# One load for the first modulation weights, fewer warm-up matmuls, a cast moved ahead of statistics, and a branch hint in a fused attention and MLP block

## The chip, the cores and the metric

One core of a Trainium2 chip. The metric is the device time of one execution in microseconds; each kernel was run several times. Executions of one kernel agree to about 0.1%, which is 1 us here (nine of the kernel before in one round: 1328.14 to 1329.20 us), and the whole change is about effects of that size. So two things are used throughout: runs of the kernel before made in the same rounds on the same chip, and the trace, in which a shift can be followed step by step.

## The reference, cut to what matters

```python
mod = (silu(c) @ w_mod).reshape(1, 6, 1, 512)        # sa, ca, ga, sb, cb, gb
h = layernorm(x) * (1 + ca) + sa                     # x: 1 x 2048 x 512
q = h @ wq                                           # 32 query heads of 128
o = softmax(q @ k.T * 128**-0.5) @ v                 # 8 KV heads, 2048 keys, from a cache
x = x + ga * (o @ wo)
h = layernorm(x) * (1 + cb) + sb
x = x + gb * mlp(h)                                  # GELU, layernorm, spatial gate, 512 -> 1792 -> 512
```

Inputs and output are bfloat16. The scores can be exponentiated without a running maximum as long as they are small; a flag computed on the way says whether that holds, and a branch at the end goes to a general path when it does not. In these runs the flag is zero and the branch jumps over that path.

## The kernel before

The change touches the first 25 us and the last matmul. The first loads: the first two of the six modulation parts (`wmod_a`, 1 MB) come in two halves, then half of K for the first head, then `wq` of the first group and the next three row tiles of x. ACT's queue issues `c` and the first row tile.

```python
    c_bf = res.tile([P, NDT], BF16, name="c_bf")
    nc.scalar.dma_start(out=c_bf[:], in_=c_dram)
    nc.scalar.dma_start(out=x_sb[:, 0, :], in_=x_dram[:, 0, :])
    for i in range(2):
        part = slice(i * D, (i + 1) * D)
        nc.sync.dma_start(out=wmod_a[:, :, part], in_=wmod_dram[:, :, part])
    k_nat = early.tile([P, SK], BF16, name="kT")
    nc.sync.dma_start(out=k_nat[:, 0:HK].rearrange(...), in_=k_rows)
    # ... (cut)
    load_wq(0, nc.sync)
    nc.sync.dma_start(out=x_sb[:, 1:CT, :], in_=x_dram[:, 1:CT, :])
```

The first row tile. `warm(n)` issues n matmuls of zeros, 128x512, which serve nothing but TensorE's clock. `mod_columns` is 32 matmuls of one column. `ln1_turn` transposes the normalised rows on TensorE and applies the modulation on DVE and ACT (the result is `hT`). `qproj` is the query projection: 16 matmuls, then a cast from PSUM to `qT`, half on DVE and half on ACT for this first tile.

```python
    warm(14)
    xns0 = ln1_norm(0, 1, ln1_stats(0, 1))
    mod_columns(0, wmod_a, 0)
    ln1_turn(0, 1, xns0, on_act=(1, 3))
    # ... K transposed on TensorE into kT0 (cut)
    warm(2)
    first = {}
    first["r1"] = ln1_stats(1, 1)
    # ... (cut: definition of qproj)
    for fn in qproj(0, list(range(REP)), 0, P, two_engines=True):
        fn()
    first["x1"] = ln1_norm(1, 1, first["r1"])
    first["r2"] = ln1_stats(2, 2)
```

Then comes the attention loop, one slot for each pair of score matmuls of 512 columns with an exponential of 1024 columns behind it. Work of the next row tiles is placed into slots by number: `at` runs it at a slot, `fill` puts matmuls between.

```python
    def first_turn():
        ln1_turn(1, 1, first["x1"])
        first["x2"] = ln1_norm(2, 2, first["r2"])

    at(0, 1, first_turn)
    at(0, 4, lambda: ln1_turn(2, 2, first["x2"]))
    fill[0, 0] = [lambda: warm(1)]
    fill[0, 2] = [lambda: warm(1)]
    fill[0, 3] = qproj(0, list(range(REP)), P, P)
    rest_q = qproj(0, [0, 1], 2 * P, 2 * P) + qproj(0, [2, 3], 2 * P, 2 * P)
    fill[0, 6], fill[0, 7], fill[1, 0] = rest_q[0:4], rest_q[4:10], rest_q[10:16]
```

## Time and profile before

| | before |
|---|---|
| time, median of 3 runs | 1328.81 us (1328.66 to 1328.84) |
| profiled span | 1326.9 us |
| TensorE busy | 98% of the span |
| granted clock, mean | 0.998 |
| first query projection | 9.62 to 10.69 us |
| first score matmul | 12.33 us |
| last of the early casts of qT | 22.98 us |

How to read the profile: PE is TensorE (PEld its weight loads), DVE VectorE, ACT ScalarE, POOL GpSimd, and SP SyncE, for which the page lists no busy time: here it issues and waits; PSUM is the memory in which the results of the matmuls lie. An engine is seen here to take its instructions in order, so one that waits holds up all behind it: the cast at 11.48 stood behind statistics, though its projection had ended at 10.69. Each line of the timeline has the start, the length, the engine, the source line, the operation with what it writes and reads, the number of instructions, and in brackets the idle time before it with what ended it. Matmuls of one group overlap in the trace (one of 512 columns is shown 0.38 us long, two 0.59); their spacing tells the clock: those of 512 columns start 427 ns apart in the warm-up before and 215 ns apart at the first score matmuls, those of 128 columns 107 and 56 ns. The lines on which the argument rests are in the prediction below.

### The profile page before, as it was taken

Reading aid. Unit: us, or ns where it says so; the run is one execution under the profiler, and the core shown is the slowest. Engines: PE = TensorE matmul, PEld = TensorE weight load, DVE = VectorE, ACT = ScalarE, POOL = GpSimd, SP = SyncE. Lnnn points to the kernel's source line nnn. Section 1 sums busy time; section 2 is a strip of 40 time slices with the busy share of each in tenths; the row PEclk is TensorE's granted clock in tenths of the full one; section 3 lists DMA queues with packets and bytes.
Section 4 is the critical chain, followed back from the end, with each engine's and each line's share of the span. In section 5 each row is a group of like instructions: output and inputs, shape, how many; then the busy total and the mean of one; then the engine's idle time right before and its main releaser. Section 6 shows DMA issues by size and latency. Waiting matters only on the chain.

```text
span 1326.9 us, 27682 instructions
## 1 busy us (share of the span) xinstructions
PE 1303.0 (98%) x12140; PEld 859.3 (65%) x12346; DVE 472.7 (36%) x1166; ACT 1077.4 (81%) x1061; POOL 48.8 (4%) x92
## 2 busy tenths in 40 slices
PE   8999999999999999999999999999999999999997
PEld 5666666666666666666666666666666666644444
DVE  5532222222222222222222222222222566793444
ACT  5898999999999999999999999999999999650000
POOL 1100000000000000000000000000000000120000
PEclk9999999999999999999999999999999999999999
DMA  5461021102111121111110211121101111154200
GB/s 159 102 146 29 17 49 37 33 17 53 21 30 36 34 37 37 29 37 37 33 33 17 53 37 29 21 52 21 33 14 21 25 34 33 29 115 83 64 21 27
DMA packets 146512, 57.59 MB, mean 43 GB/s; under 512 B 136176, under 2 KB 142448, under 8 KB 146384
## 3 DMA queue, kind: packets, MB, share of 16 engines
q1 hardware_dynamic: 139584, 37.19, 14.8%
q0 software_dynamic: 4208, 16.39, 4.5%
q8 instruction: 98, 1.61, 0.5%
q10 hardware_dynamic: 2592, 2.16, 0.5%
q14 instruction: 30, 0.25, 0.1%
HBM read 21.37 MB, written 2.10 MB: 18 GB/s over the span
## 4 chain that ended last, share of the span: by engine, by line
PE 97%; issue 1%; DVE 1%; DMA 1%; ACT 0%; SPq 0%; POOL 0%
PE s_ps L928 35%; PE o_ps L950 35%; PE misc L1290 7%; PE misc L889 7%; PE misc L982 6%; PE s_ps L1136 2%; PE s_ps L1175 2%; PE o_ps L1311 1%; DMA x_sb<-in_A_x_dram 1%; PE s_ps L1311 0%; DVE bnst L691 0%; ACT pT L935 0%; PE misc L1052 0%; DVE qT L901 0%; DVE xn L680 0%
## 5 line engine op out<-in xcount | busy, mean ns | idle before, releaser
L935 ACT ACTIVATE pT<-s_ps 128x1024 bf16<-128x1024 f32 x1024 | 1043.6, 1024 | 86.0 <-PE s_ps L928 11.3
L950 PEld LDWEIGHTS <-pT 128*128 128x128 bf16 x8192 | 548.5, 98 | 241.2
L950 PE MATMUL o_ps<-v,pT 128*128 128x129 bf16 x8192 | 631.5, 220 | 0.0
L928 PE MATMUL s_ps<-qT,kT 128*128 128x512 bf16 x2048 | 608.9, 379 | 12.4 <-ACT qT L903 1.6
L961 DVE RECIPROCAL rall<-o_ps 128x2 f32<-128x2 f32 x256 | 43.6, 170 | 743.9 <-PE o_ps L950 743.8
L928 PEld LDWEIGHTS <-kT 128*128 128x128 bf16 x2048 | 199.3, 98 | 121.8 <-issue 3.6
L889 PE MATMUL misc<-hT,wq_g 128*128 128x512 bf16 (+2 forms) x482 | 167.4, 365 | 0.2
L982 PE MATMUL misc<-wo_g,oT 128*128 128x512 bf16 x385 | 145.9, 379 | 0.0
L962 DVE TENSOR_TENSOR onorm<-o_ps,rall 128x256 bf16<-128x256 f32 x256 | 108.6, 424 | 9.0 <-DVE rall L961 0.3
L1290 PE MATMUL misc<-wsp,z 128*128 128x512 bf16 (+2 forms) x555 | 100.5, 336 | 0.6 <-issue 0.3
L901 DVE CAST qT<-misc 128x512 bf16<-128x512 f32 (+1 forms) x128 | 86.7, 677 | 7.4 <-PE misc L889 7.3
L1290 PEld LDWEIGHTS <-z 128*128 128x128 bf16 x560 | 50.6, 98 | 48.5
L995 DVE TENSOR_TENSOR xacc<-misc,xacc 128x512 f32<-128x512 f32 x112 | 76.0, 679 | 0.0
L889 PEld LDWEIGHTS <-wq_g 128*128 128x128 bf16 x544 | 51.5, 98 | 1.5 <-DMA wq_g<-in_A_wq_dram 0.6
L982 PEld LDWEIGHTS <-oT 128*128 128x128 bf16 x512 | 50.1, 98 | 0.7
L1305 DVE TENSOR_TENSOR gb<-misc,bsp_bc 128x512 bf16<-128x512 f32 (+1 forms) x28 | 18.4, 658 | 59.2 <-PE misc L1290 59.2
L1136 PE MATMUL s_ps<-win_sb,hT 128*128 128x448 bf16 x128 | 27.0, 352 | 0.1
L1146 ACT ACTIVATE z<-s_ps 128x896 bf16<-128x896 f32 x16 | 14.7, 917 | 14.9 <-PE s_ps L1136 14.9
L1175 PE MATMUL s_ps<-hT,win_sb 128*128 128x512 bf16 x109 | 24.3, 379 | 0.2
L691 DVE BATCH_NORM_STATS2 bnst<-x_sb 128x6 f32<-128x512 bf16 x32 | 21.8, 682 | 3.1 <-DMA x_sb<-in_A_x_dram 2.6
L1183 ACT ACTIVATE z1T<-s_ps 128x1024 bf16<-128x1024 f32 x14 | 14.3, 1024 | 10.1 <-PE s_ps L1175 9.1
L708 POOL DMA_DIRECT2D wq_g<-in_A_wq_dram x7 | 5.3, 750 | 420.9 <-PE misc L889 420.9
(79 smaller groups left out, 280.1 us busy)
## 6 DMA issues: line engine op xcount, KB each, us to landing
wq_g<-in_A_wq_dram POOLq DMA_DIRECT2D x7, 512.0 KB, 4.0
v<-in_A_v_cache_dram POOLq DMA_DIRECT2D x7, 512.0 KB, 6.5
wo_g<-in_A_wo_dram POOLq DMA_DIRECT2D x7, 512.0 KB, 4.8
oT<-onorm SPq DMA_TRANSPOSE x128, 2.4
wsp<-in_w_mod_dram POOLq DMA_DIRECT2D x1, 2048.0 KB, 9.3
out_dram<-yout ACTq DMA_DIRECT2D x15, 128.0 KB, 1.7
win_sb<-in_B_w_in_dram POOLq DMA_DIRECT2D x1, 1792.0 KB, 7.7
x_sb<-in_A_x_dram SPq DMA_DIRECT2D x3, 512.0 KB, 6.1
```

The costliest lines, as they stand in the source:

```text
L889: nc.tensor.matmul(ps[0][:, o0 : o0 + n], lhsT=wqs[g][:, dt, hh * DH : (hh + 1) * DH], rhs=hTs[ch][:, dt, c0 : c0 + n], start=(dt == 0), s ...
L901: nc.vector.tensor_copy(out=dst[:, 0:cut], in_=src[:, 0:cut])
L928: nc.tensor.matmul(s_ps[:, h * 512 : (h + 1) * 512].rearrange("p (r q) -> p r q", r=REP), lhsT=groups[g]["kT"][:, kt * P : (kt + 1) * P], ...
L935: nc.scalar.activation(out=pTs[u][:, 2 * i : 2 * i + 2, :], in_=s_ps[:].rearrange("p (k q) -> p k q", k=2), func=ACT.Exp, scale=inv_sqrt_dh,)
L950: nc.tensor.matmul(o_ps[:, hh % 2, 0 : DH + 1], lhsT=pTs[u][:, kt, hh * P : (hh + 1) * P], rhs=groups[g]["v1"][:, kt, 0 : DH + 1], start=( ...
L961: nc.vector.reciprocal(out=rall[:, c0 : c0 + 2], in_=o_ps[:, :, DH])
L962: nc.vector.tensor_tensor(out=onorms[u][:, hh - 1 : hh + 1, :], in0=o_ps[:, :, 0:DH], in1=rall[:, c0 : c0 + 2].unsqueeze(2).to_broadcast([ ...
L982: nc.tensor.matmul(X_ps[:], lhsT=oTs[u][:, hh, :], rhs=groups[g]["wo"][:, hh, :], start=(hh == 0), stop=(hh == REP - 1),)
L995: nc.vector.tensor_tensor(out=xaccs[j][:], in0=X_ps[:], in1=xaccs[j][:], op=ALU.add)
L1136: nc.tensor.matmul(ps[0][:, hf * 512 : hf * 512 + FC], lhsT=h2Ts[j // CT][:, dt, (j % CT) * P : (j % CT + 1) * P], rhs=win_sb[:, dt, FH + ...
L1175: nc.tensor.matmul(ps[0][:, k * 512 : (k + 1) * 512], lhsT=win_sb[:, dt, f * P : (f + 1) * P], rhs=h2Ts[2 * ch2 + k][:, dt, :], start=(dt ...
L1290: nc.tensor.matmul(g_ps[:, :n], lhsT=z2[:, st, f * P : (f + 1) * P], rhs=wsp[t][:, st, c0 : c0 + n], start=(st == 0), stop=(st == NT - 1 a ...
```

## The change

Its intent: to bring the first score matmul forward. One load in place of two saves an issue (the two take SyncE's queue 1.36 us before); three warm-up matmuls fewer free TensorE (427 ns each); the first cast of `qT` no longer stands behind the statistics of the next tile on DVE; the work of the next tiles is shifted to slots where its data are there; and the last branch is marked as likely taken, in the hope of a shorter branch (3.65 us on TensorE's sequencer before).

```diff
-    for i in range(2):
-        part = slice(i * D, (i + 1) * D)
-        nc.sync.dma_start(out=wmod_a[:, :, part], in_=wmod_dram[:, :, part])
+    nc.sync.dma_start(out=wmod_a[:], in_=wmod_dram[:, :, 0 : 2 * D])
@@
-    warm(14)
+    warm(11)
@@
     warm(2)
-    first = {}
-    first["r1"] = ln1_stats(1, 1)
@@ behind the first qproj
+    first = dict(r1=ln1_stats(1, 1))
+    ln_stats(mv1, 2, x_sb[:, 2, :])
     first["x1"] = ln1_norm(1, 1, first["r1"])
-    first["r2"] = ln1_stats(2, 2)
+    ln_stats(mv1, 3, x_sb[:, 3, :])
+    first["r2"] = rstd_of(mv1[:, 2:4, :], 2, "ln1")
@@
-    at(0, 1, first_turn)
-    at(0, 4, lambda: ln1_turn(2, 2, first["x2"]))
-    fill[0, 0] = [lambda: warm(1)]
-    fill[0, 2] = [lambda: warm(1)]
-    fill[0, 3] = qproj(0, list(range(REP)), P, P)
+    at(0, 3, first_turn)
+    at(0, 5, lambda: ln1_turn(2, 2, first["x2"]))
+    for i in range(3):
+        fill[0, i] = [lambda: warm(1)]
+    fill[0, 4] = qproj(0, list(range(REP)), P, P)
@@
+    tc.mark_branch_hint_location("redo", "LikelyTaken")
     o2_mm(o2_last[CT - 1], yT, CT - 1, NFT - 1)
@@
-    with tc.If(redo != 0):
+    with tc.If(redo != 0, label="redo"):
```

## The prediction

> **What bounds the kernel now.** I read the busy shares and the shares of the chain that ended last first, then the timeline of the first 31 us (all of the diff but one mark lies there), then the instructions of the branch that closes the program.
>
> ```profile
> PE 1303.0 (98%) x12140; PEld 859.3 (65%) x12346; DVE 472.7 (36%) x1166; ACT 1077.4 (81%) x1061; POOL 48.8 (4%) x92
> ...
> PE 97%; issue 1%; DVE 1%; DMA 1%; ACT 0%; SPq 0%; POOL 0%
> ```
>
> Matmuls fill 98% of a span of 1326.9 us and 97% of the chain. The diff leaves the attention loop and the MLP as they are, so what can move is the head, where the PE waits for first data, and the few microseconds behind the last matmul. The time on record (1328.81 us) lies 1.9 us above the profiled span; I take that offset as constant.
>
> The head, from the timeline of the kernel before (start and length in us, engine, line, what, count, and in brackets the idle time before it with what ended it):
>
> ```profile
> 1.18 5.98 PE L768 MATMUL o_ps<-onorm 128*128 128x512 bf16 x14 [1.18 <-DVE onorm L750]
> ...
> 6.99 1.00 PE L784 MATMUL misc<-sc_bf,wmod_a 128*128 128x1 bf16 x32
> ...
> 8.75 0.81 ACT L844 ACTIVATE hT<-misc,modc 128x128 bf16<-128x128 bf16 x2 [5.63 <-DVE hT L817]
> ...
> 9.62 0.90 PEld L889 LDWEIGHTS <-wq_g 128*128 128x128 bf16 x16 [0.63 <-DMA wq_g<-in_A_wq_dram]
> 9.62 1.07 PE L889 MATMUL misc<-hT,wq_g 128*128 128x128 bf16 x16
> ...
> 10.65 0.69 DVE L691 BATCH_NORM_STATS2 bnst<-x_sb 128x6 f32<-128x512 bf16 x1 [1.66 <-DMA x_sb<-in_A_x_dram]
> ...
> 11.48 0.39 DVE L901 CAST qT<-misc 128x256 bf16<-128x256 f32 x1
> ...
> 11.90 0.37 ACT L903 CAST qT<-misc 128x256 bf16<-128x256 f32 x1 [1.45 <-DVE qT L901]
> ...
> 12.33 0.59 PE L928 MATMUL s_ps<-qT,kT 128*128 128x512 bf16 x2 [1.64 <-ACT qT L903]
> ...
> 17.31 0.38 PE L835 MATMUL misc<-ident,xn 128*128 128x128 bf16 x4 [0.42 <-DVE qT L901]
> ...
> 18.16 4.73 ACT L935 ACTIVATE pT<-s_ps 128x1024 bf16<-128x1024 f32 x5 [1.39 <-PE s_ps L928]
> ```
>
> To see here: the first query projection (L889) runs from 9.62 to 10.69. Its cast should follow at once, but DVE executes in order, and ahead of the cast stand the statistics of the next row tile (L691), whose data came at 10.65. So the cast starts at 11.48, ACT's half at 11.90, the first score matmul at 12.33; the PE idles 1.64 us. From then on ACT sets the pace of the first eight exponentials (about 1.02 us each), with one hole of 1.39 us before 18.16: the PE, also in order, stands at a transpose (17.31) whose PSUM buffer waits for a qT cast.
>
> The chain in order of time shows that a delay here is handed on. The last early qT cast (22.98) is followed by the statistics of the second chunk, and the PE waits for what comes of them:
>
> ```profile
> 22.98 0.69 DVE qT L901
> 23.67 0.61 DVE bnst L691
> ...
> 28.35 1.39 DVE xn L680 x4
> 29.79 0.90 PE misc L835 x13
> ```
>
> The tail, from the instructions of L1378 (last columns: length in ns, first and last start in us):
>
> ```profile
> L1378 SPq EVENT_SEMAPHORE  x8: 17/17/17, 1324.6 to 1325.2; - x8
> ...
> L1378 PEldq COMPARE_BRANCH  x1: 3651/3651/3651, 1319.7 to 1319.7; - x1
> ...
> L1378 SPq COMPARE_BRANCH  x1: 53/53/53, 1321.6 to 1321.6; - x1
> ```
>
> The branch around the fallback took the PE's sequencer 3.65 us; SP's ended at 1321.7 and its next instruction came at 1324.6, 2.9 us later. The last landing of an output transfer was at 1323.6, so the branch costs the end about 1.0 to 1.5 us.
>
> [...]the PE starts at half clock and goes to full[...]: the warm-up matmuls of 512 columns follow each other at 427 ns until 6.70, and the step after that one is 294 ns, so the change came near 6.86, after 5.7 us of activity. [...]Here packets of 1024 B took 52 ns on average and those of 2048 B (few) 84 ns[...].
>
> **The change part by part.**
>
> 1. *One load of wmod_a in place of two.* One issue on SP of 0.6 to 0.7 us goes, and rows come in pieces of 2 KB. From the trace's packets: 1 MB over 16 engines is 64 packets of 52 ns (3.35 us) or 32 of 84 ns (2.70 us), 0.65 us less DMA work ahead of K, wq_g and x. The DMA engines are saturated from 3 us on, so most of that should reach wq_g: its landing at 9.58 goes to about 9.1. The other side: all 32 column matmuls now need the whole load. Before, its halves landed at 5.33 and 7.40, and the 17th matmul stood until then; I expect one landing near 6.7.
>
> 2. *11 warm-up matmuls in place of 14.* 3 x 0.427 = 1.28 us of PE time goes, so warm-up ends at about 5.9 and the columns start when wmod_a lands, 6.7, ending at about 7.5 in place of 8.0. The normalised input of the first tile (done at 7.19) is ready by then. ACT's part of hT, which ended at 9.56, ends at about 9.1. Both gates of the projection thus move by some 0.5 us: it runs from 9.1 to 10.2.
>
> 3. *The cast ahead of the statistics.* It starts when the projection ends. Before, 11.48 - 10.69 = 0.79 us lay between them. With 0.39 us for DVE's half, 0.37 for ACT's and the same small gaps, the first score matmul goes to 12.33 - 0.5 - 0.77, about 11.05. The statistics lose nothing: they start when x lands, near 10.1 to 10.6.
>
> 4. *The first turn in slot 3, the second in slot 5, the projection of tile 1 in slot 4.* I laid out the slots by the durations above. The first exponential starts at 11.7, its followers run back to back, and the second tile's normalised rows (about 13.0) and hT (about 15.0) are ready before slots 3 and 4 want them. The hole stays, as projection, cast and second turn still stand next to each other: cast from 16.3 to 17.0, score matmul of slot 5 at 17.25, exponential at 17.9. But five exponentials lie before it now and not four. Before, the sixth started at 18.16 + 1.02 = 19.18; now at 17.9. That is 1.28 us, the shift of parts 1 to 3 and nothing beyond. The extra warm-up matmul in slot 1 (0.22 us at full clock) lies in PE waiting time.
>
> 5. *The hint.* In the built program no engine has a hint instruction: matmuls and weight loads fall by two each (three fewer, one more), SP has one transfer less and DVE one wait less; nothing else changes in number. The mark names no engine and leaves nothing behind. I count 0 us, and the branch keeps its stall.
>
> Sum: 0.5 (wq_g and hT) + 0.77 (cast) = 1.27 us at the first score matmul and, with some loss, 1.25 us at the cast of 22.98. Behind that all waits are relative to earlier work, so it is kept to the end: 1328.81 - 1.25 = 1327.55.
>
> **The rivals.**
>
> *The clock comes late.* [...]Now full-size matmuls stop at 5.9 and there is a gap to about 6.7. [...]the projection takes 16 x 107 in place of 16 x 56 ns (0.8 us more) and the first pair of scores 0.4 us more; the later pairs hide behind exponentials. That eats the gain: 1328.5 to 1329. [...]About one in four.
>
> *The loads gain nothing.* If a single transfer only moves the bytes about and wq_g still lands at 9.6, parts 1 and 2 give 0 and the cast alone remains: 1328.0. The saturated DMA engines speak for this, the packet times against. Nearly one in four.
>
> *The hint works after all*, being placed outside the program I read. Then SP waits for its last landing only: 1.0 to 1.5 us more, 1326.0 to 1326.5. Against it: no such instruction is there. One in twenty.
>
> *The slots lengthen the hole*, because the later second turn delays the third and fourth tiles' projection and the PE's first value matmuls: up to 0.5 us back. By my layout the transposes wait for nothing new.
>
> **Range and chances.** Centre 1327.5. Below, better loads by half a microsecond, or the hint, reach 1326.6. Above, the late clock reaches 1328.6. Repeats differ by 0.2 us. A gain of 2% would be 26 us, of which there is no trace.
>
> **What would show it right or wrong.** Right: the cast of qT directly behind the first projection, the first score matmul near 11.0 and the last early cast near 21.7; one hole in the exponentials of 1 to 1.4 us, after the fifth; wq_g landing near 9.1; the PE's branch still above 3 us. Part 1 is wrong if the projection still waits for wq_g to 9.5; part 2 if its matmuls follow each other at 107 ns; part 5 if a hint instruction appears and SP's gap behind the branch is gone. The whole is wrong if the shift at 22 us does not equal the shift of the total.

The sum is 0.5 (load) + 0.77 (cast) = 1.27 us at the first score matmul and 1.25 us at the cast of 22.98. The DMA share that it calls saturated is 0.87 from 3 to 4 us in the trace before, and 1.05 to 1.11 from 4 to 9.

## The result, and the profile after

| | before | after |
|---|---|---|
| time, median (range), 6 runs each | 1328.74 us (1328.37 to 1329.28) | 1328.96 us (1327.58 to 1329.5) |
| ratio, 95% interval | | 1.0001 [0.9988, 1.0014] |
| profiled span | 1326.87 us | 1327.02 us |

A ratio is always the mean time of one kernel's runs over the mean of the other's runs in the same rounds, so it is not quite the ratio of the medians quoted. The result is correct, and the time is the same: none of the 1.25 us that I had predicted came. But the spread of the new kernel is wider, and one of its runs is a full microsecond faster than the others.

The head in the timeline of the kernel after, the same steps as shown of before:

```profile
1.18 4.50 PE L766 MATMUL o_ps<-onorm 128*128 128x512 bf16 x11 [1.18 <-DVE onorm L748]
...
6.97 0.95 PE L782 MATMUL misc<-sc_bf,wmod_a 128*128 128x1 bf16 x32 [1.29 <-DMA wmod_a<-in_w_mod_dram]
...
8.71 0.81 ACT L842 ACTIVATE hT<-misc,modc 128x128 bf16<-128x128 bf16 x2 [5.59 <-DVE hT L815]
...
9.02 1.06 PE L766 MATMUL o_ps<-onorm 128*128 128x512 bf16 x2
...
9.87 1.91 PE L885 MATMUL misc<-hT,wq_g 128*128 128x128 bf16 x16
...
11.82 0.42 DVE L897 CAST qT<-misc 128x256 bf16<-128x256 f32 x1 [2.89 <-PE misc L885]
...
12.70 0.59 PE L927 MATMUL s_ps<-qT,kT 128*128 128x512 bf16 x2 [0.92 <-ACT qT L899]
...
19.35 3.81 ACT L934 ACTIVATE pT<-s_ps 128x1024 bf16<-128x1024 f32 x4 [1.34 <-PE s_ps L927]
...
23.25 0.69 DVE L897 CAST qT<-misc 128x512 bf16<-128x512 f32 x1 [1.07 <-PE misc L885]
```

Two things went as wanted. The cast (11.82) now follows the projection directly, and among the first eight exponentials there is one hole, of 1.34 us, after the fifth and not after the fourth. But the projection itself (L885) takes 1.91 us where it took 1.07: its 16 matmuls stand 107 ns apart, not 56. The two warm-up matmuls ahead of it (9.02) stand 427 ns apart, where two at full clock stand 215 ns apart, and push its start from 9.62 to 9.87. So the first score matmul comes at 12.70, later than before (12.33).

Busy time by stretches of 1 us tells why. The columns are the stretch, its length, the busy time of PE, PEld, DVE, ACT and POOL with counts in brackets, then the granted clock, the share of the DMA engines, and GB/s.

```profile
5.00:6.00 1.00, 0.68 (x3) 0.14 (x1) 0.39 (x1) 0.00 (x0) 0.00 (x0) 1.00 1.06 407
6.00:7.00 1.00, 0.03 (x1) 0.04 (x2) 0.49 (x2) 0.00 (x0) 0.30 (x2) 1.00 1.04 390
...
8.00:9.00 1.00, 0.99 (x12) 0.87 (x13) 0.78 (x4) 0.29 (x1) 0.00 (x0) 0.79 1.10 349
9.00:10.00 1.00, 1.00 (x7) 0.44 (x5) 0.00 (x0) 1.00 (x3) 0.00 (x0) 0.50 1.24 235
```

The clock's own records in the trace say: up at 5.18 us, back to half at 8.59, full again at 12.00. So the clock was not late; it came up at 5.18 and fell back for 3.41 us, over just the stretch in which the first projection lies. In the window before, TensorE stands from 5.7 to 6.97 waiting for `wmod_a`, and behind that wait come 32 matmuls of a single column, which fill 0.95 us of busy time with next to no columns. By my count of streamed columns the window from 5.18 to 8.59 was filled to 0.26 (an estimate: the columns divided by 1.2 a nanosecond at half clock, which is 512 in 427 ns, and by twice that at full, where the trace has 512 in 215 ns). Before, with 14 warm-up matmuls, the clock came up at 6.85 and stayed up to 1320.98, behind the last matmul.

The tail, as in the prediction: the instructions of the closing branch (length in ns three times, first and last start in us).

```profile
L1378 SPq EVENT_SEMAPHORE  x8: 17/17/17, 1324.8 to 1325.3; - x8
...
L1378 PEldq COMPARE_BRANCH  x1: 3547/3547/3547, 1319.9 to 1319.9; - x1
...
L1378 SPq COMPARE_BRANCH  x1: 53/53/53, 1321.9 to 1321.9; - x1
```

Nothing has changed here: 3.55 us of TensorE's sequencer (3.65 before), and 2.9 us between SyncE's branch and its next instruction.

### The profile page after: what moved, and what is told of

It reads as the page before. It is cut to its first block, busy times and chain, and to the rows that moved or that the text cites. A ratio compares the mean times of both kernels' runs of the same rounds, so it can differ in the third digit from the quotient of the medians.

```text
span 1327.0 us, 27882 instructions
## 1 busy us (share of the span) xinstructions
PE 1314.0 (99%) x12344; PEld 860.0 (65%) x12344; DVE 473.3 (36%) x1166; ACT 1077.3 (81%) x1061; POOL 49.2 (4%) x92
## 4 chain that ended last, share of the span: by engine, by line
PE 98%; DVE 1%; DMA 0%; ACT 0%; POOL 0%; issue 0%; ACTq 0%
PE o_ps L949 35%; PE s_ps L927 33%; PE misc L885 8%; PE misc L981 8%; PE misc L1289 7%; PE s_ps L1135 2%; PE s_ps L1174 2%; PE o_ps L1310 1%; PE s_ps L1310 1%; DMA x_sb<-in_A_x_dram 0%; ACT pT L934 0%; DVE bnst L691 0%; DVE qT L897 0%; DVE xn L680 0%; PE misc L833 0%; PE misc L1051 0%
## 5 line engine op out<-in xcount | busy, mean ns | idle before, releaser
L981 PE MATMUL misc<-wo_g,oT 128*128 128x512 bf16 x512 | 194.0, 379 | 0.0
L885 PE MATMUL misc<-hT,wq_g 128*128 128x512 bf16 (+2 forms) x544 | 191.2, 369 | 0.0
L885 PEld LDWEIGHTS <-wq_g 128*128 128x128 bf16 x544 | 52.3, 99 | 1.4 <-DMA wq_g<-in_A_wq_dram 0.3
```

The costliest lines, as they stand in the source:

```text
L885: nc.tensor.matmul(ps[0][:, o0 : o0 + n], lhsT=wqs[g][:, dt, hh * DH : (hh + 1) * DH], rhs=hTs[ch][:, dt, c0 : c0 + n], start=(dt == 0), s ...
L981: nc.tensor.matmul(X_ps[:], lhsT=oTs[u][:, hh, :], rhs=groups[g]["wo"][:, hh, :], start=(hh == 0), stop=(hh == REP - 1),)
```

## The experiments

Sixteen kernels ran, and each gave the correct result. "Before" beside each is the median of the kernel before on the same chip and in the same rounds. The three of one look each are used for their traces alone. Only the intervals of `best2` and `best3` leave out 1: every other difference of medians is inside the noise and stands or falls with the traces.

| run | time us, median (range) | before | ratio [95%] | last early cast | span |
|---|---|---|---|---|---|
| a_again | 1329.14 (1328.64 to 1330.52) | 1328.43 | 1.0007 [0.9993, 1.0021] | 23.20 | 1326.98 |
| a_warm14 | 1327.57 (1327.45 to 1329.09) | 1328.43 | 0.9996 [0.9982, 1.0010] | 22.02 | 1325.76 |
| b_cast | 1329.77 (1328.63 to 1331.3) | 1328.43 | 1.0011 [0.9998, 1.0025] | 22.98 | 1326.85 |
| a_hint | 1328.66 (1327.48 to 1329.06) | 1328.43 | 1.0002 [0.9988, 1.0015] | 21.88 | 1325.63 |
| b_slots | 1328.28 (1328.21 to 1328.52) | 1328.24 | 1.0000 [0.9986, 1.0014] | 22.55 | 1326.47 |
| b_warm11 | 1328.66 (1327.97 to 1330.28) | 1328.24 | 1.0004 [0.9990, 1.0018] | 23.95 | 1327.88 |
| b_cast_slots | 1327.93 (1327.61 to 1329.36) | 1328.24 | 0.9999 [0.9985, 1.0013] | 22.29 | 1326.14 |
| a_hint_inv | 1327.44 (1327.23 to 1329.38) | 1328.24 | 0.9999 [0.9985, 1.0013] | 21.69 | 1325.60 |
| b_load | 1327.99 (1327.88 to 1328.6) | 1328.25 | 0.9998 [0.9984, 1.0012] | 22.59 | 1326.54 |
| best1 | 1327.57 (1327.41 to 1328.05) | 1328.25 | 0.9995 [0.9981, 1.0009] | 21.98 | 1325.78 |
| best2 | 1326.11 (1326.03 to 1326.32) | 1328.25 | 0.9984 [0.9970, 0.9997] | 24.25 | 1324.24 |
| a_hint_static | 1327.84 (one look) | 1328.25 | | 23.63 | 1325.95 |
| b_hint_static | 1326.78 (1326.46 to 1327.71) | 1328.45 | 0.9990 [0.9977, 1.0004] | 22.50 | 1324.71 |
| best3 | 1324.60 (1324.54 to 1324.82) | 1328.45 | 0.9971 [0.9958, 0.9985] | 24.25 | 1322.81 |
| a_hint_mid | 1330.90 (one look) | 1328.45 | | 21.85 | 1329.10 |
| a_hint_mid1 | 1332.21 (one look) | 1328.45 | | 24.75 | 1330.42 |

Names with a start from the kernel after the change, names with b from the kernel before.

### The clock: a_again, a_warm14, b_warm11

The theory after the first result: 11 warm-up matmuls let the clock fall back over the projection. The rival: the gain is lost elsewhere, in the loads or the slots. `a_again` is the changed kernel once more, unedited.

> The changed kernel once more. Clock theory: what the change wins in the head is lost when the PE's clock falls back to half for one or more windows of 3.4 us before 14 us, at random from run to run. So times scatter from 1327.5 to 1329.5 and follow the mean granted clock: 0.998 near 1327.6, 0.997 near 1328.8, 0.996 near 1329.4. Rival (late first row tile: its load lands at 5.6 us in place of 4.8 and gates everything): times lie together near 1328.9 whatever the clock.

Measured: 1329.14 us, and in its profile again a half-clock stretch, here from 7.92 to 11.33, behind a window that was filled to 0.23. The projection again takes 1.67 us. The five times follow the mean clock, as expected and against the rival of a late row tile: 0.997 at 1328.64 to 1329.14, 0.996 at 1329.37, 0.995 at 1330.52; and the fast run of the first result, 1327.58, is the only one there at 0.998.

`a_warm14` has one edit:

```diff
-    warm(11)
+    warm(14)
```

> The changed kernel with 14 warm-up matmuls in place of 11. Clock theory: with about 1 us more of full-size matmuls before the wmod_a load lands the clock stays full after it has come up; no half-clock stretch before 14 us, first projection ends near 10.6, first score matmul near 11.5, time 1327.7 to 1328.1. Rival (late first row tile): the same time as the changed kernel, 1328.9.

Measured: 1327.57 us, 1.57 us less than the same kernel with 11. Its clock at the stretch of the projection, in the columns as above:

```profile
6.00:7.00 1.00, 1.00 (x4) 0.25 (x2) 0.38 (x2) 0.00 (x0) 0.41 (x2) 1.00 1.05 391
...
9.00:10.00 1.00, 1.00 (x14) 0.69 (x12) 0.04 (x1) 1.00 (x3) 0.00 (x0) 1.00 1.18 232
```

TensorE is now busy until `wmod_a` is there, and the clock stays at 1.00. The first score matmul comes at 11.47 and the last early cast at 22.02. One of its five runs, at 1329.09 us, has a mean clock of 0.997, lower than the others (0.998 and 0.999) by about what one half-clock stretch costs by my estimate (half of 3.41 us in 1327, 0.0013). So 14 seem to make the fallback rarer (one run of five at 0.997 or less, for 16 of 21 with 11, below), not impossible; no trace of that run was kept.

`b_warm11` is the reverse, the kernel before with 11 in place of 14:

```diff
-    warm(14)
+    warm(11)
```

> The kernel before with 11 warm-up matmuls in place of 14, nothing else. Clock theory: the PE stands between about 5.5 and the landing of wmod_a's second half at 7.4 except for 16 small matmuls, so the window after the clock came up is too empty: mean granted clock 0.997 or lower in most runs and 0.3 to 1 us slower than before, with a wider scatter. Rival (warm-up count does not matter, the landing gates all): same time, clock 0.998.

Measured: in its profile the clock comes up at 5.50 and falls back from 8.92 to 15.74, for 6.82 us, twice 3.41. The timeline of that kernel:

```profile
7.19 0.55 PE L784 MATMUL misc<-sc_bf,wmod_a 128*128 128x1 bf16 x16 [0.96 <-DMA wmod_a<-in_w_mod_dram]
...
9.38 1.89 PE L889 MATMUL misc<-hT,wq_g 128*128 128x128 bf16 x16
```

The wait of 0.96 us for the second half of `wmod_a` and then the slow projection: the same picture, without any other part of the change. So the smaller warm-up alone was enough for a fallback. The median, 1328.66, is only 0.42 us above the kernel before, because the five runs fall into two kinds: 1327.97 to 1328.66, at mean clocks of 0.999 to 0.997, and 1329.76 (the profiled one, at 0.996) and 1330.28. The last has a mean clock of 0.998; a clock that came up late, as in `a_hint_mid1` below, would show that way, but it has no trace. What sets the two kinds apart was read across the traces.

The clock's changes lie 3.41 us or a whole number of times that apart: 5.18, 8.59 and 12.00 in the kernel after, 7.92 and 11.33 in `a_again`, 8.92 and 15.74 in `b_warm11`, and 6.85 and 1320.98 before (385 times 3.413). The first of them came at 4.50 to 6.85, and in `a_hint_mid1` at 17.1. So I cut each trace into windows of 3.41 us from there, forwards and back. The windows behind which the clock fell were filled to 0.17, 0.23, 0.26 and 0.37 by my count; all others at full clock, from 0.42 up, were followed by full clock, except those at the end of each trace, where the matmuls stop: filled to 0.38 at most, they were followed by half. TensorE's plain busy time does not tell them apart: it was 1.78 to 2.26 us of 3.41 in the four windows of a head behind which the clock fell, and 1.75 in one behind which it held (`b_hint_static`, from 9.53). As to the rise, no window at half clock filled to 0.71 or less was followed by full clock, one at 0.73 was and one at 0.74 was not, and all from 0.80 up were. The changed head fell back in the traces in which the clock had come up at 4.50, 5.05 and 5.18, and held in those in which it came up at 6.26, 6.47 and 6.77.

So the time at which the clock comes up is a rival of the number of warm-up matmuls, and the traces tell the two apart. With 14, the clock came up at 4.60 (`b_slots`), 4.88 (`b_cast`) and 5.46 (`b_load`), the window from there was filled to 0.47 to 0.50, and the clock held. With 11 it came up at 4.50, 5.05, 5.18 and 5.50 (`b_warm11`), the window was filled to 0.17 to 0.37, and it fell. The times agree: of the 21 timed runs of the changed head with 11 (the result, `a_again`, `a_hint`, `a_hint_inv`) five have a mean clock of 0.998 and lie at 1327.23 to 1327.58 us, and the others have 0.997 or less and lie at 1328.27 to 1330.52; with 14 (`a_warm14`) it is four of five at 1327.45 to 1327.76.

### The parts by themselves: b_cast, b_slots, b_cast_slots, b_load

`b_cast` moves only the statistics behind the first cast (the diff's third part), `b_slots` only the slots (its fourth), `b_cast_slots` both, each on the kernel before with its 14 warm-up matmuls and two loads.

> The kernel before with only the cast of qT put ahead of the statistics. Clock theory: here the clock is as before, so the 0.77 us between projection and first score matmul are won and kept: first score matmul at 11.6, time 1328.0 against 1328.75 before. Rival (the later statistics delay the second tile's turn, which stands in slot 1 here, by as much): same time as before.

> The kernel before with only the slots moved (first turn 3, second 5, projection of tile 1 in slot 4, one more warm-up matmul). Theory (cast and slots are worth something only together): the score matmul of 12.33 stays, five exponentials run from 13.0 to 18.1, the cast of tile 1 ends near 18.2 and the sixth exponential starts near 19.1, against 19.18 before: time as before within 0.3 us. Rival (the slots are what the gain comes from): 0.8 us faster.

> The kernel before with the cast moved and the slots moved; two loads of wmod_a and 14 warm-up matmuls stay. If the gain is cast and slots together and the single load gives nothing: first score matmul near 11.4, hole after the fifth exponential, 1327.4 to 1327.7, equal to the changed kernel with 14 warm-up matmuls. If the single load gives half a microsecond as the prediction had it: 1328.0.

Measured: `b_cast` is not faster (1329.77 for 1328.43; the slowest run, 1331.3, has a mean clock of 0.996, and two more have 0.997, so part of this median is probably lost clock, with 14 warm-up matmuls; only the fastest run was profiled). Its profile, in which the clock held, has the span of the kernel before, though the first cast starts at 10.38 for 11.48, 0.34 of it by an earlier landing of `wq`. The exponentials in its timeline show where the gain goes:

```profile
13.97 2.85 ACT L936 ACTIVATE pT<-s_ps 128x1024 bf16<-128x1024 f32 x3 [1.05 <-PE s_ps L929]
...
18.16 4.73 ACT L936 ACTIVATE pT<-s_ps 128x1024 bf16<-128x1024 f32 x5 [1.34 <-PE s_ps L929]
```

There is a new hole of 1.05 us behind the first exponential, as TensorE now reaches the second tile's transposes in slot 1 before their rows are ready, and the fifth exponential starts at 18.16, to the hundredth where it started before. `b_slots` alone gives nothing either (1328.28 for 1328.24), as the first cast still stands 0.83 us behind the projection's end (11.15 and 10.32). Together they have a span of 1326.14 us and a median of 1327.93, 0.31 us below the kernel before: the cast's gain is kept only if the slots move with it. In its profile the span is 0.73 us below, though `wq` landed 0.1 us later than in the kernel before.

`b_load` takes only the single load:

```diff
-    for i in range(2):
-        part = slice(i * D, (i + 1) * D)
-        nc.sync.dma_start(out=wmod_a[:, :, part], in_=wmod_dram[:, :, part])
+    nc.sync.dma_start(out=wmod_a[:], in_=wmod_dram[:, :, 0 : 2 * D])
```

> The kernel before with one part of the change: the modulation weights are loaded by one DMA in place of two halves. My theory (the load trades one landing for another): the tokens of the first tile land about 0.7 us later than before (5.4 to 5.6 for 4.83), the rest earlier by one issue (wq at 9.0 to 9.2 for 9.58), so the first projection ends within 0.3 us of the kernel before and the median is within 0.3 us of it, if the clock is at full speed throughout (mean 0.998 or more). The rival, from my prediction (one issue less is 0.45 to 0.5 us off everything): 0.5 us faster, last early cast at 22.5 for 22.98.

Measured: 1327.99 for 1328.25, 0.26 us less and inside the interval. As the theory had it, the load trades one landing for another:

```profile
5.61 0.69 DVE L691 BATCH_NORM_STATS2 bnst<-x_sb 128x6 f32<-128x512 bf16 x1 [1.67 <-DMA x_sb<-in_A_x_dram]
...
9.27 1.19 PE L887 MATMUL misc<-hT,wq_g 128*128 128x128 bf16 x16
```

The first row tile, which another queue issues, landed at 5.59 and not at 4.83, so its statistics start at 5.61; `wq` landed at 9.13 and not at 9.58. The projection starts 0.35 us earlier but takes 1.19 us, as its later matmuls wait for ACT's half of `hT`, which ends at 9.52 where it ended at 9.56.

### Repairing the head: best1, best2

`best1` is the changed kernel with 14 warm-up matmuls and fillers in the two waits that follow, so that in its profile no window is filled to less than 0.62 by my count:

```diff
-    warm(11)
+    warm(14)
@@ behind mod_columns
+    warm(1)
@@ behind the first qproj
+    warm(3)
```

> The changed kernel with 14 warm-up matmuls in place of 11, and a few more of them in the two waits that follow (one after the modulation columns, three after the first projection), so that no stretch of 3.4 us has TensorE streaming less than 0.44 of the time. My theory of the clock: no run of it has a half-speed stretch after the clock came up (every mean clock 0.998 or more), last early cast at 21.9 to 22.1, span 1325.6 to 1325.9, median 1327.3 to 1327.7. Rival (the fallback depends on something else[...]): some of the five runs at 0.997 or less, as with the 14 alone, where one in five was.

Measured: 1327.57 us, the same median as `a_warm14`, and no run with a mean clock below 0.998. Five of five runs of the one and four of five of the other do not tell 14 with fillers from 14 without, but with `best2` and `best3`, which have the same fillers, fifteen runs of fifteen held their clock (mean 0.998 or more).

`best2` adds to it:

```diff
-    at(0, 5, lambda: ln1_turn(2, 2, first["x2"]))
+    at(0, 6, lambda: ln1_turn(2, 2, first["x2"]))
-    fill[0, 6], fill[0, 7], fill[1, 0] = rest_q[0:4], rest_q[4:10], rest_q[10:16]
+    fill[0, 7], fill[1, 0], fill[1, 1] = rest_q[0:5], rest_q[5:10], rest_q[10:16]
```

> As the run above (14 warm-ups and fillers), and the second turn of the modulation one slot later (at slot 6 for 5), with the rest of the projection spread over the slots in sixes. If the hole of 1.34 us in front of the sixth exponential is the second turn and the rest of the projection standing in front of a score matmul in TensorE's order, it goes or shrinks: last early cast 20.7 to 21.6, median 1325.5 to 1326.9. Rival: the hole is bound by the cast behind the statistics of the later tiles, and only moves: median as in the run above, within 0.3 us, with a hole of 1.0 to 1.4 us after another exponential.

Measured: 1326.11 us, 1.46 below `best1`. The time is as expected, the position of the last early cast is not: 24.25, because the statistics of the second chunk now run before it. The exponentials:

```profile
16.79 4.02 ACT L936 ACTIVATE pT<-s_ps 128x1024 bf16<-128x1024 f32 x4 [0.17 <-PE s_ps L929]
...
22.63 4.69 ACT L936 ACTIVATE pT<-s_ps 128x1024 bf16<-128x1024 f32 x5 [0.52 <-PE s_ps L929]
28.63 2.89 ACT L936 ACTIVATE pT<-s_ps 128x1024 bf16<-128x1024 f32 x3 [1.31 <-PE s_ps L929]
```

The hole after the fifth exponential is 0.17 us in place of 1.33, and the wait at 28.63 is 1.31 us where `best1` and the kernel before have 2.15. A new one of 0.28 us appears in between, so not all of the 2.0 us arrives at the end.

### The hint: a_hint, a_hint_inv, a_hint_static

The mark of the change names no engine, and the built program has no hint instruction. So I gave it the four engines that take the long branch. With a register's value (the flag, loaded before) it stays where it is written, just before the last matmul (TensorE's at 1317.19 in `a_hint`); with the fixed "LikelyTaken" the built program has it at the start of each engine's program. `a_hint` is the first form:

```diff
-    tc.mark_branch_hint_location("redo", "LikelyTaken")
+    redo = nc.values_load(flag[0:1, 0:1], min_val=0, max_val=P)
+    tc.mark_branch_hint_location("redo", redo, engines=[PE, Activation, DVE, SP])
```

> The changed kernel with a hint that exists: the flag is loaded to registers ahead of the last matmul and a hint from that register follows on PE, ACT, DVE and SP. If the fetch is what the tail waits for: PE's branch falls from 3.5 us to under 1, SP's gap behind its branch from 2.9 to 1 to 2 us (then its last landing holds it), time 1.0 to 1.5 below the changed kernel of the same rounds. Rival (the hint changes nothing, or the loads of the flag delay the last matmul): same time or 0.3 more.

Measured: 1328.66 us for 1328.43. The hint ran on TensorE at 1317.19, 0.8 us before the branch, which took 3.69 us all the same. `a_hint_inv` turns the condition of the branch round, so that the same value says the opposite:

```diff
-    with tc.If(redo != 0, label="redo"):
-        general_path(...)
+    with tc.If(redo == 0, label="redo", preferred_fallthrough_block=False) as cmp:
+        pass
+    with cmp.Else():
+        general_path(...)
```

> The changed kernel with a register hint as before, but the branch turned round: on flag equal to zero it goes to the empty arm, which lies behind the fallback. If the first hint did nothing because it meant the arm that follows at once: now instruction fetches appear after the hints and ahead of the branches, PE's branch falls under 1 us, and from the last output issue to the end of the span it takes 4.0 to 4.5 us in place of 5.5. Rival (a hint has no effect here): fetches stay behind the branches, 5.5 us.

Measured: TensorE's branch 3.14 us, SyncE's gap 3.0 us, nothing gained at the tail. Both profiles have a span of 1325.6 us, but that comes from their heads: the clock had come up at 6.77 and 6.26 and held.

At that point I held a hint to be without effect here. `a_hint_static` was to close the matter with the fixed form:

```diff
-    tc.mark_branch_hint_location("redo", "LikelyTaken")
+    tc.mark_branch_hint_location("redo", "LikelyTaken", engines=[PE, Activation, DVE, SP])
```

> The changed kernel with the hint given the four engines by name and no register, which puts the hint as the first instruction of each of the four engines' programs. Theory (a hint has no effect on this tail): no instruction is fetched ahead of the branches, the first fetch of the tail starts about 0.9 us after a branch, TensorE's branch takes 3 us or more, and from the last output's issue to the end there are 5.4 to 5.8 us. Rival (the place decides): the fetch starts ahead of the branch and the tail is 2 to 3 us shorter.

Measured: my theory fell. The instructions of its branch:

```profile
L1378 SPq EVENT_SEMAPHORE  x8: 17/17/17, 1322.8 to 1324.2; - x8
...
L1378 PEldq COMPARE_BRANCH  x1: 407/407/407, 1320.3 to 1320.3; - x1
...
L1378 SPq COMPARE_BRANCH  x1: 73/73/73, 1322.3 to 1322.3; - x1
```

TensorE's branch takes 0.41 us in place of 3.55, and SyncE goes on 0.5 us after its own. From the issue of the last output to the end there are 4.09 us where the kernel after has 5.54. Its head had the half-clock stretch (granted 0.73 from 8 to 9 us and 0.50 from 9 to 11), so the time of 1327.84 is one of a slow head and a fast tail. The instruction fetches, in the page's list of DMA queues (packets, MB, share), are:

```profile
q8 instruction: 97, 1.59, 0.5%
...
q14 instruction: 27, 0.22, 0.1%
```

The kernels before and after have 98 and 30. In the trace's record of each fetch, the ordinary ones come at the same times in both kernels (the last of TensorE's queue near 1311 us), there is none extra ahead of the branch, and behind each branch there is one where there were two (before: 16 KB at 1320.68 and 1324.08 behind TensorE's branch, six of 8 KB from 1322.26 to 1325.46 behind the other three). From these counts I infer that the target comes in place of the last ordinary fetch; what a fetch holds, no trace shows. That would explain the failure of `a_hint`: there the last ordinary fetch was at 1309.32, and the hint came at 1317.19.

### Place or form: a_hint_mid, a_hint_mid1, b_hint_static, best3

`a_hint_mid` has the form by register again, but directly behind the computation of the flag, 77 us before the branch; `a_hint_mid1` the same with the flag plus one.

```diff
                 check_flag()
+                redo = nc.values_load(flag[0:1, 0:1], min_val=0, max_val=P)
+                tc.mark_branch_hint_location("redo", redo, engines=[PE, Activation, DVE, SP])
```

> The changed kernel with the hint by register (the flag, zero here), placed at once behind the flag's computation: on TensorE some 930 instructions ahead of the branch, so ahead of that engine's last ordinary fetch near 1310 us. If the place decides, TensorE's branch takes about 0.4 us and its fetch of 16 KB behind the branch goes, here or in the run with the value one, whichever polarity says taken. Rival (the form decides): 3 us or more in both.

> As the run before it, with the flag plus one in the register, so the value one. Theory (place): of the two runs, one has TensorE's branch near 0.4 us, and an engine whose hint still comes behind its last ordinary fetch keeps its stall. Rival (form): 3 us or more in both.

Measured, with the value zero:

```profile
L1379 SPq EVENT_SEMAPHORE  x8: 17/17/17, 1326.8 to 1327.4; - x8
...
L1379 PEldq COMPARE_BRANCH  x1: 410/410/410, 1321.6 to 1321.6; - x1
```

TensorE's hint ran at 1244.27 and its last ordinary fetch came at 1313.07: the branch takes 0.41 us. On the other three engines the hint ran at the same time, but the last ordinary fetch of the queue that serves them was at 1238.0, before it: there are still six fetches on it behind their branches, and SyncE still waits from 1324.1 to 1326.8. With the value one:

```profile
L1379 PEldq COMPARE_BRANCH  x1: 3766/3766/3766, 1322.9 to 1322.9; - x1
```

The full stall. So with the register form too the branch can be short, 0.41 us from a place ahead of the last ordinary fetch where it was 3.69 in `a_hint`, and zero is the value that made it so here. Both runs are slower as a whole, 1330.9 and 1332.2 us; their spans less the last early cast are 3.4 and 1.8 us above that of the kernel before. TensorE now loads the flag in the middle of the program and stands for 1.89 us at 1242.5 waiting for it; in the first run its clock fell for a window behind that, at 1245.5. The second had a misfortune of its own in the head, of which below.

`b_hint_static` is the kernel before with nothing but the fixed hint, `best3` is `best2` with it.

> The kernel before with nothing but the fixed hint, the four engines named, at the start of each engine's program. Theory (the fetch of the target takes the place of the last ordinary fetch): TensorE's branch about 0.4 us, one fetch of 16 KB and three of 8 KB less than before, SyncE's next instruction after its branch within 0.6 us, from the last output's issue to the end 3.9 to 4.4 us for 5.6, so the median 1.2 to 1.7 us below before. Rival (the gain of the last run came from its head, not its tail): within 0.4 us of before.

> The best version so far (14 warm-ups and fillers, second turn at slot 6) with the fixed hint at the start. If head and tail are independent, its median is that of the best version less what the hint alone gives: 1324.4 to 1325.0, all clocks at 0.998 or more. Rival (with an earlier end of the tail, another wait closes the program, such as the landing of the last output): 1325.2 to 1325.9.

Measured: 1326.78 us for 1328.45, so 1.67 us for the hint alone; two of the five runs, 1327.65 and 1327.71, gained only 0.8, at a mean clock of 0.998 where the other three have 0.999 or 1.000. The interval still includes 1, but the trace agrees: the distance from the last early cast to the end of the span, 1303.9 us in the kernel before, is 1302.2 here, with one fetch of 16 KB and three of 8 KB fewer, as expected. `best3` has 1324.60 us, 1.51 below `best2` in its own rounds, and its five runs lie within 0.3 us: head and tail add. It is 3.85 us or 0.29% faster than the kernel before, and the best version.

## Why the prediction was wrong, point by point

The prediction was 1327.5 us with a range of 1326.6 to 1328.6; measured were 1328.96. The direction of four of the five parts was right, and the step that failed is the second.

1. *One load (predicted 0.5 us at both gates).* The size was wrong. `wq` moved from 9.58 to 9.14, but 9.58 was a late one: it landed at 9.06 to 9.70 in the six traces with two loads (mean 9.35) and at 8.94 to 9.37 in the twelve with one (mean 9.10), so the load brings 0.26. The packets of 2 KB took 96 ns in the kernel after (640 of them), not the 84 that I had from a few; with that, 64 x 52 less 32 x 96 ns is 0.26 us and not 0.65. And I had kept the first row tile's normalised input at 7.19, and it moved to 7.95, as the row tile, on another queue, landed 0.76 us later with the single load (5.59 for 4.83; in all traces 5.35 to 5.82 with one load, 4.70 to 4.91 with two). Whether the larger pieces did it or the larger load, no run tells. ACT's half of `hT` ended at 9.52, where I expected 9.1. At full clock, in `a_warm14`, the projection's last matmul starts at 10.33 for 10.47: the term of 0.5 measures 0.14 us in this pair, and 0.06 between the means of the traces at full clock (10.25 in five with two loads, 10.19 in eight with one).

2. *Eleven warm-up matmuls (predicted: TensorE time that is free).* This is the step that failed. Three fewer left TensorE waiting for 1.29 us just after its clock came up at 5.18, the window from there was filled to 0.26, and the clock went back to half from 8.59, over the first projection. The first cast starts at 11.82 where it starts at 10.58 with 14: 1.24 us, the whole of the predicted gain. The traces with 14 whose clock came up at such times (4.60 to 5.46) and the times of `a_warm14` show that it is this number, and `b_warm11` that nothing else of the change is needed for it. The five runs in which the clock held with 11 lie at the predicted time, 1327.23 to 1327.58, and 0.8 to 1.2 us below the kernel before of their rounds; that they hit it so closely is partly luck, as the term of part 1 was too large. My first rival had the right consequence, a projection at 107 ns a matmul and 1328.5 to 1329 us, at one chance in four. But its mechanism, a clock that comes late, is not what the result shows: it came up at 5.18, 1.7 us earlier than before, and fell at 8.59. I had asked whether the clock would come up in time and not whether it would stay up. A late clock was seen as well: in `a_hint_mid1`, with the same head, four windows in a row filled to 0.68 to 0.70 passed without a rise, and the clock stayed at half until 17.1 us, which made that profile's last early cast the latest of all, 24.75. Its mean clock of 0.999 does not show it, as the profile has 1.00 up to the first change, although the matmuls follow each other at half clock there (107 ns in the projection at 10.10).

3. *The cast ahead of the statistics (predicted 0.77 us).* Right. In `a_warm14` the first cast is 0.90 us earlier than before, of which 0.14 are the projection's: 0.76. That it needs the slots of part 4 to be kept was not in the prediction; `b_cast` showed it.

4. *The slots.* Right: five exponentials before the hole, one hole of 1.34 us, nothing gained by themselves. What I took as given, that the hole stays, was the larger chance: one slot later for the second turn, and it goes (`best2`, 1.46 us). One reading was off: the sixth exponential of the kernel before started at 19.08, not 19.18, as they follow each other at 0.92 us and not at their length of 1.02.

5. *The hint (predicted 0 us).* Right, for the reason given: no instruction. The value of a hint that works, 1.0 to 1.5 us in the rivals, measures 1.67 (1.5 on top of `best2`).

6. *A shift at 22 us is the shift of the total.* Right. In the kernels before and after and the first eight experiments the span less the last early cast lies between 1303.7 and 1303.9 us. It is why so small a cause shows at the end of 1.3 ms.

With the terms measured in this pair of traces the sum at the first cast is 0.14 + 0.76 - 1.24 = -0.34 us, a loss; in the traces it is 11.48 to 11.82.

## What to carry to other kernels

A warm-up is not only for reaching the full clock. In these traces the clock fell back when the next 3.41 us were filled to 0.37 or less by my count, and held from 0.42 up; with the warm-up extended until the first real matmuls had their data and fillers in the waits behind it, all fifteen runs had a mean clock of 0.998 or more (`best1` to `best3`). When a head is a chain of small gains, look at which part of the change can undo the rest before summing them, and test the parts together with what they need: the cast here is worth nothing without the slots. A branch hint must be in the built program. In these runs it shortened TensorE's branch only where it ran before the last ordinary fetch ahead of it (0.41 us in `a_hint_static`, `b_hint_static`, `best3` and, with the value zero, `a_hint_mid`), and not behind that fetch (3.69 and 3.14 us in `a_hint` and `a_hint_inv`); check the hint instruction's count and the branch's length, not the source line.
